# The last chunk's low weights in both halves of the rows, and the first balance's small matmuls inside the projection

## The chip, the cores and the metric

One core of one Trainium2 chip. The metric is the device time of one execution in microseconds (us). Of the kernel before, three runs took 2725.89 to 2726.05 us, median 2726.04.

## The reference

x is 2048 rows of 576. Two attentions with 32 heads of 18 read the same x; a sigmoid gate per row mixes them:

```python
g = _sigmoid((x * gate_w).sum(-1, keepdims=True))
a = _A_ref(x, A_wqkv, A_wo)              # softmax attention, own k and v for each head
b = _B_ref(x, B_wq, B_wk, B_wv, B_wo)    # one k and one v for all heads
return g * a + (1 - g) * b
```

## The kernel before

The work has two parts. The first part projects x with all weights; the second runs, for 64 heads, a pass for the row maxima (L511), the scores with their exponentials (L548, L555) and the product with v (L561), and at times the output projection (L677). The change touches the first part alone.

**Projection.** The weights that act on the columns of q, k, the gate and B's v stand side by side as 14 tiles of 128 columns. x comes transposed, in chunks of 128 of its 576 rows: four full chunks and a last one of 64 rows. A product of two f32 numbers is made of three products of rounded ones: every operand is split into a high part (`h`) and a low part (`l`, the rest). One accumulation over all chunks is written out in `PROJ` (L37): four matmuls high by high, four with low weights by high x, four with high weights by low x, and two for the last chunk. There x keeps its high part in partitions 0 to 63 and its low part in 64 to 127 of the same chunk (L332, L334), and the high weights are written into both halves (L135), so that one matmul on 128 rows gives two of the products. The low weights of that chunk are written into rows 0 to 63 alone (L137), and the fourteenth matmul has 64 rows.

A *job* is one such accumulation for a weight tile and 512 columns of x: 14 tiles by 4 are 56 jobs, number 0 to 55 (`JOBS`). Tiles 0 to 2 come first, in turns over the columns (jobs 0 to 11), then tiles 3 to 13 with four jobs each. Jobs 0 to 2 are made in two halves of 256 columns each, as x arrives. A job writes one bank of PSUM; three banks are named `ps`, four `pm`, and jobs take them by threes (L236). ScalarE and VectorE empty a bank later (`evict`: L248, L251, L254, for some also L257 to L260) into high and low f16 parts, scaled by a column of `tv`; GpSimd issues their transfers. VectorE and ScalarE also split x as it comes (L331 to L334, 256 columns at a time), and split the weights (L133 to L137): for tiles 0 to 2 and v's weights the subtractions are VectorE's, for tiles 3 to 13 they are GpSimd's (`eng_l`).

**Balance.** `tv` comes from the sizes of the weights. For the first three tiles: VectorE measures the weights of five tiles (L173), takes the maximum (`br`, L197); TensorE turns it (L205, the turn of br); VectorE makes `bd` of it (L207 to L210); TensorE spreads `bd` to all partitions (L213); VectorE computes `tv` (L215 to L225). `balance` is a generator with a stop behind `br` and one behind `bd`. It runs beside jobs 3, 4 and 5; the evictions of jobs 0 to 5 follow it. Job 6 uses the bank of job 0 and columns of x that are split behind job 0's eviction. The second balance (`br` at L202) stands around jobs 13 to 15, behind ten measurements of VectorE (L186 to L191).

**V jobs.** 32 projections of A's v (L289, the same fourteen matmuls, 288 columns, x as the stationary operand) end the first part. They alternate with the first max matmuls (L511, 54 rows, alternately in partitions 64 to 117 and 0 to 53).

The engines work through their instructions in the order in which the program writes them.

Of the kernel before, what the change touches and what calls it, by code (L numbers as in the profile page):

```python
# [8 lines left out]
F32 = mybir.dt.float32  # L9
# [5 lines left out]
OP = mybir.AluOpType  # L15
# [9 lines left out]
NKT = 5  # L25
# [9 lines left out]
LEAD = 22  # L35
PRODS = (("h", "h"), ("h", "l"), ("l", "h"))
PROJ = [("h", "h", k, 128) for k in range(NKT - 1)] + [("l", "h", k, 128) for k in range(NKT - 1)] + \  # L37
       [("h", "l", k, 128) for k in range(NKT - 1)] + [("h", "h", NKT - 1, 128), ("l", "h", NKT - 1, 64)]


def q_row(u):
# [8 lines left out]
def gated_mix_kernel(ctx: ExitStack, tc: tile.TileContext, xT, wall, wv, wo, out):  # L50
    nc = tc.nc
# [75 lines left out]
    def load5(t, src, eng=None):  # L127
        dma(t[:, 0:4, :], src[0:512, :].rearrange("(k p) m -> p k m", p=P), eng)
        dma(t[0:64, 4, :], src[512:576, :], eng)

    def split_w(st, w, eng_l):

        nc.scalar.activation(w["h"][:, 0:4], st[:, 0:4], AF.Copy)  # L133
        for b in (0, 64):
            nc.scalar.activation(w["h"][b:b + 64, 4], st[0:64, 4], AF.Copy)  # L135
        eng_l.tensor_tensor(w["l"][:, 0:4], st[:, 0:4], w["h"][:, 0:4].bitcast(F32), op=OP.subtract)
        eng_l.tensor_tensor(w["l"][0:64, 4], st[0:64, 4], w["h"][0:64, 4].bitcast(F32), op=OP.subtract)  # L137

    norm_b = wpool.tile([P, 2, 10], F32, name="norm_b", bufs=1)
    norm_a = wpool.tile([P, (MT - 4) * P], F32, name="norm_a", bufs=1)  # L140
# [19 lines left out]
    def turn_mask():  # L160
        pt = ps_m.tile([P, 512], F32, name="pm")
        for g in range(4):
            nc.tensor.transpose(pt[:, MT * g:MT * g + MT], mask_r[:, g, :], ident[0:MT, 0:MT])
        nc.vector.tensor_copy(mask, pt[:, 0:4 * MT].rearrange("p (g m) -> p g m", m=MT))

    def load_w(mt, eng=None):
        st = wpool.tile([P, NKT, P], F32, name="wst", bufs=MT - 2)
        load5(st, wall[mt], eng)
        return st
# [6 lines left out]
    def measure_b(mt, st):  # L176

        if mt == 0:
            size(norm_b[:, 0, 0:2], st[:, :, ROW_KB:ROW_KB + DH])
        f0, f1 = max(ROW_Q - P * mt, 0), min(ROW_Q + DH * H - P * mt, P)  # L180
        size(norm_b[:, 1, 2 * mt:2 * mt + 2], st[:, :, f0:f1])
# [45 lines left out]
    def prep_w(st, eng=None):  # L227
        w = {y: wpool.tile([P, NKT, P], F32R, name=f"w{y}", bufs=4) for y in "hl"}
        split_w(st, w, eng or nc.gpsimd)
        return w  # L230
# [4 lines left out]
    def bank(odd=False):  # L235
        return ps_m.tile([P, 512], F32, name="pm") if odd else ps_s.tile([P, 512], F32, name="ps")  # L236

    def products(fp, w, s0, a0, b0):
        for n, (a, b, k, kr) in enumerate(PROJ):
            nc.tensor.matmul(fp[:, a0:b0], w[a][:kr, k, :], X[b][:kr, k, s0 + a0:s0 + b0],  # L240
                             start=(n == 0), stop=(n == len(PROJ) - 1), skip_group_check=True)

    def evict(mt, c, fp):
        cs = slice(c * 512, (c + 1) * 512)
        h = stp.tile([P, 512], F16, name="ph")
        l = stp.tile([P, 512], F16, name="pl")
        t = tv[:, mt:mt + 1]
        nc.scalar.activation(h, fp, AF.Copy, scale=t)  # L248
        if mt == 0 or c == 0 and mt in HAS_K:
            st = stp.tile([P, 512], F32, name="pst", bufs=3)  # L250
            nc.scalar.activation(st, fp, AF.Copy)  # L251
            if c == 0:
                KD[mt] = st
        nc.vector.scalar_tensor_tensor(l, fp, t, h, op0=OP.mult, op1=OP.subtract)  # L254
        if c == 1 and mt in HAS_K:
            d = stp.tile([P, 512], F32, name="pd", bufs=1)
            nc.vector.tensor_tensor(d, fp, KD.pop(mt), op=OP.subtract)  # L257
            dh, dl = (stp.tile([P, 512], F16, name=f"pd{y}", bufs=1) for y in "hl")
            nc.scalar.activation(dh, d, AF.Copy, scale=t)
            nc.vector.scalar_tensor_tensor(dl, d, t, dh, op0=OP.mult, op1=OP.subtract)  # L260
        dma(qk_d[0][mt * P:(mt + 1) * P, cs], h, nc.gpsimd)
        dma(qk_d[1][mt * P:(mt + 1) * P, cs], l, nc.gpsimd)
        if c == 1 and mt in HAS_K:
            dma(kd_d[0][mt * P:(mt + 1) * P, :], dh, nc.gpsimd)
            dma(kd_d[1][mt * P:(mt + 1) * P, :], dl, nc.gpsimd)
        if mt == 0:
            dma(z_d[cs], st[ROW_G:ROW_G + 1, :], nc.gpsimd)
            ST[c] = st
# [3 lines left out]
    def shared_v(c):  # L272
        st = ST.pop(c)
        pv = ps_m.tile([P, 512], F32, name="pm")
        for j in range(4):
            nc.tensor.transpose(pv[:, 18 * j:18 * j + 18],
                                st[ROW_VB:ROW_VB + 18, j * P:(j + 1) * P],
                                ident[ROW_VB:ROW_VB + 18, ROW_VB:ROW_VB + 18])
        nc.vector.tensor_copy(vb[:, 4 * c:4 * c + 4, 0:18],
                              pv[:, 0:72].rearrange("p (j d) -> p j d", d=18))  # L280
# [14 lines left out]
    def run(gen):  # L295
        for _ in gen:
            pass
# [6 lines left out]
    def flush():  # L304
        for f in list(late):
            late.remove(f)
            f()

    def project(n, hold=False):

        mt, c = JOBS[n]
        fp = bank(n // 3 % 2)
        products(fp, WP[mt], 512 * c, 0, 512)
        if not hold:
            flush()
        late.append(lambda: evict(mt, c, fp))
        if mt == 0:
            late.append(lambda: late.append(lambda: shared_v(c)))

    with tc.tile_pool(name="xs", bufs=6, side="right") as xsp:  # L320
        XS = []

        def load_x(c, eng=None):
            XS.append(xsp.tile([P, NKT, 256], F32, name="xs"))
            load5(XS[c], xT[:, 256 * c:256 * c + 256], eng)

        def split_x(c):
            xs = XS[c]
            cs = slice(c * 256, (c + 1) * 256)
            xh, xl = X["h"][:, :, cs], X["l"][:, :, cs]  # L330
            nc.scalar.activation(xh[:, 0:4], xs[:, 0:4], AF.Copy)  # L331
            nc.scalar.activation(xh[0:64, 4], xs[0:64, 4], AF.Copy)  # L332
            nc.vector.tensor_tensor(xl, xs[:, 0:4], xh[:, 0:4].bitcast(F32), op=OP.subtract)
            nc.vector.tensor_tensor(xh[64:128, 4], xs[0:64, 4], xh[0:64, 4].bitcast(F32), op=OP.subtract)  # L334

        W = [load_w(0)]
        load_x(0, nc.scalar)
        early = qs[2][:, 0:512]
        nc.vector.memset(early, 0.0)
        nc.scalar.activation(qs[1][:, 0:32], ones, AF.Copy, scale=0.0)  # L340
        for _ in range(18):
            nc.tensor.matmul(acc, early[:, 0:P], early, start=True, stop=True)
        W.append(load_w(1))
        load_x(1)
        W.append(load_w(2))
        for c in (2, 3):
            load_x(c)
        W += [load_w(3), load_w(4)]
        for c in (4, 5):
            load_x(c)  # L350
        WP = [prep_w(W[0], nc.vector)]
        split_x(0)
        for mt in (1, 2):
            WP.append(prep_w(W[mt], nc.vector))
        split_x(1)
        FP = [bank() for mt in range(3)]
        for i in range(2):
            for mt in range(3):
                products(FP[mt], WP[mt], 0, 256 * i, 256 * i + 256)
        for mt in range(3):  # L360
            measure_b(mt, W[mt])
        for c in (2, 3):
            split_x(c)
        turn_mask()
        for c in (6, 7):
            load_x(c)
        for mt in range(5, MT):
            W.append(load_w(mt))
        for mt in (3, 4):
            measure_b(mt, W[mt])  # L370
        project(3, hold=True)
        bal = balance(0)
        for n in (4, 5):
            next(bal)
            project(n, hold=True)
        run(bal)
        for mt in range(3):
            evict(mt, 0, FP[mt])
            if mt == 0:
                for c in (4, 5):  # L380
                    split_x(c)
        flush()
        WP.append(prep_w(W[3]))
        shared_v(0)
        for n in range(6, 12):
            if n == 8:
                for c in (6, 7):
                    split_x(c)
            project(n)
            for mt in range(*AT.get(n, (0, 0))):  # L390
                measure_a(mt, W[mt])
# [355 lines left out]
    at = {}  # L747
# [49 lines left out]
    for T in range(-LEAD, NSTEP + 2, 2):  # L797
# [11 lines left out]
        for op in order.split():  # L809
            k, second, c = op[0], op[1:2] == "B", op[2:]  # L810
# [67 lines left out]
```

## Time and profile before

| | |
|---|---|
| median of 3 runs | 2726.04 us |
| the profiled execution | 2726.16 us, span 2724.3 |
| TensorE busy | 2689.0 us, 99% of the span |
| VectorE | 2421.9 us, 89% |
| ScalarE | 2389.5 us, 88% |
| GpSimd | 285.7 us, 10% |
| mean granted TensorE clock | 0.995 |
| jobs 0 to 55 | 8.96 to 224.68 us |
| V jobs, with the first max matmuls | 224.68 to 306.6 us |

The span goes from the first instruction to the last; the execution's own time has 1.9 us around it. PE is TensorE's matmuls, PEld its weight loads, DVE VectorE, ACT ScalarE, POOL GpSimd. A row of the timeline gives start, duration, engine, line, operation and, for matmuls, rows by columns of the stationary operand and the moving one; rows alike are merged (x4 at the end), and then the duration is that of the whole group. Matmuls are pipelined, so that the durations of neighbours overlap: starts are to be read. In the chain of work that ended last, each piece is what the next one waited for.

### The profile page before, as it was taken

The page shows a single profiled execution, that of the slowest core. Times are in us where ns is not written, and L with a number is a line of the kernel's source. Part 1 is how long each engine was busy: PE and PEld are TensorE (multiplying, and loading weights), DVE is VectorE, ACT ScalarE, POOL GpSimd, SP SyncE. Part 2 cuts the span into 40 slices and gives each one's busy share as a digit, 9 for nine tenths or more (in the row PEclk, how much of TensorE's full clock was granted, in tenths as well). Part 3 has the DMA queues.
Part 4 walks back from the last instruction along what each step waited for, and adds up shares of the span by engine and source line. Part 5 has one row for each costly group of instructions (what it writes and reads, how often), then busy time and mean ns, then how long its engine had stood idle before and what let it go on. Part 6 is the DMA issues. An engine that isn't in the chain of part 4 may idle for free.

```text
span 2724.3 us, 57935 instructions
## 1 busy us (share of the span) xinstructions
PE 2689.0 (99%) x22210; PEld 957.2 (35%) x22210; DVE 2421.9 (89%) x4589; ACT 2389.5 (88%) x4809; POOL 285.7 (10%) x531
## 2 busy tenths in 40 slices
PE   8999999999999999999999999999999999999999
PEld 6767522222222222222222333333333332223444
DVE  6335899999999999999999999999999999998865
ACT  4332599999999999999999999999999999998875
POOL 3641000001000200110110001000100021001000
PEclk9999999999999999999999999999999999999998
DMA  6322100002001100110132113112221112122312
GB/s 188 114 97 85 38 16 19 20 22 59 27 18 32 45 26 17 45 43 20 32 72 80 41 49 97 40 41 57 72 66 48 47 58 64 39 68 85 89 36 95
DMA packets 127089, 150.36 MB, mean 55 GB/s; under 512 B 55339, under 2 KB 94411, under 8 KB 125614
## 3 DMA queue, kind: packets, MB, share of 16 engines
q1 hardware_dynamic: 113628, 121.86, 15.8%
q0 software_dynamic: 7968, 19.23, 2.1%
q10 hardware_dynamic: 5216, 5.57, 0.6%
q8 instruction: 174, 2.85, 0.4%
q14 instruction: 103, 0.84, 0.1%
HBM read 90.89 MB, written 46.45 MB: 50 GB/s over the span
## 4 chain that ended last, share of the span: by engine, by line
ACT 50%; PE 40%; DVE 6%; DMA 2%; issue 1%; SPq 1%; POOL 0%; DVEq 0%; ACTq 0%; POOLq 0%
ACT pt L555 45%; PE acc L561 13%; PE ps L548 11%; ACT xb L514 6%; PE pm L677 4%; PE ps L240 4%; PE pm L240 4%; DVE mx L520 3%; PE ps L289 3%; PE pm L511 1%; SPq L56 1%; DMA R<-r_d 1%; DVE oe L571 1%; DVE junk L517 1%; DVE oacc L731 0%
## 5 line engine op out<-in xcount | busy, mean ns | idle before, releaser
L555 ACT ACTIVATE pt<-ps 128x512 f32<-128x512 f32 x4052 | 2093.2, 637 | 67.8 <-PE pm L511 59.8
L520 DVE TENSOR_REDUCE mx<-pm 128x1 f32<-128x512 f32 x3096 | 1941.4, 683 | 93.6 <-PE pm L511 52.8
L548 PE MATMUL ps<-qs,ksb 56*128 56x512 f16 x2688 | 818.4, 380 | 10.7
L511 PE MATMUL pm<-ksb,qs 54*128 54x512 f16 x2364 | 742.2, 383 | 2.2 <-DVE mx L520 1.1
L561 PE MATMUL acc<-pt,vb 128*19 128x512 f32 (+1 forms) x6136 | 592.2, 458 | 1.9
L561 PE MATMUL acc<-pt,vg 128*19 128x256 f32 (+1 forms) x5664 | 579.5, 481 | 2.3 <-DVE oe L571 0.5
L511 PEld LDWEIGHTS <-qs 54*128 54x128 f16 x4096 | 332.2, 93 | 245.6 <-issue 196.7
L548 PE MATMUL ps<-qs,ksa 56*128 56x512 f16 x1364 | 404.3, 379 | 4.8 <-ACT pt L555 1.3
L548 PEld LDWEIGHTS <-ksb 56*128 56x128 f16 x2688 | 175.0, 94 | 622.1 <-issue 575.8
L511 PE MATMUL pm<-ksa,qs 54*128 54x512 f16 x1232 | 384.8, 382 | 0.5 <-ACT xb L514 0.2
L517 DVE CUSTOM_DVE_ANT_0 junk<-pm,xb 128x512 bf16<-128x512 f32 x500 | 340.6, 681 | 0.0
L514 ACT ACTIVATE xb<-pm 128x512 f32<-128x512 f32 x500 | 316.6, 633 | 0.0
L548 PEld LDWEIGHTS <-ksa 56*128 56x128 f16 x1408 | 89.3, 94 | 328.8 <-issue 298.1
L530 POOL TENSOR_SCALAR mt<-mt 128x32 f32<-128x32 f32 x64 | 18.6, 290 | 1612.0 <-DVE mt L528 1612.0
L561 PEld LDWEIGHTS acc<-pt,vb 128*19 128x19 f32 x6136 | 104.1, 96 | 223.5 <-issue 206.4
L561 PEld LDWEIGHTS acc<-pt,vg 128*19 128x19 f32 x5664 | 96.1, 97 | 222.8 <-issue 204.9
L511 PE MATMUL pm<-kdb,qs 54*128 54x512 f16 x372 | 141.5, 380 | 0.0
L248 ACT ACTIVATE ph<-ps,tv 128x512 f16<-128x512 f32 x29 | 19.8, 686 | 67.3 <-PE ps L240 43.2
L292 ACT ACTIVATE vst<-ps 128x288 f32<-128x288 f32 x32 | 13.2, 412 | 67.4 <-PE ps L289 67.4
L571 DVE COPY oe<-acc 128x512 f32<-128x512 f32 x63 | 43.6, 692 | 30.0 <-PE acc L561 27.9
L248 ACT ACTIVATE ph<-pm,tv 128x512 f16<-128x512 f32 x27 | 18.4, 686 | 54.5 <-PE pm L240 40.6
L254 DVE SCALAR_TENSOR_TENSOR pl<-pm,tv,ph 128x512 f16<-128x512 f32 x27 | 20.1, 749 | 48.8 <-ACT ph L248 38.7
(151 smaller groups left out, 1518.6 us busy)
## 6 DMA issues: line engine op xcount, KB each, us to landing
qs<-qkh SPq DMA_DIRECT2D x244, 72.0 KB
qs<-qkl SPq DMA_DIRECT2D x122, 72.0 KB
onh<-oh SPq DMA_DIRECT2D x32, 256.0 KB
onl<-ol SPq DMA_DIRECT2D x32, 256.0 KB
oih<-onh SPq DMA_DIRECT2D x16, 512.0 KB
oil<-onl SPq DMA_DIRECT2D x16, 512.0 KB
ot<-oe SPq DMA_DIRECT2D x220, 36.0 KB
R<-r_d SPq DMA_DIRECT2D x55, 144.0 KB
```

The source lines that it names most:

```text
L240: nc.tensor.matmul(fp[:, a0:b0], w[a][:kr, k, :], X[b][:kr, k, s0 + a0:s0 + b0], start=(n == 0), stop=(n == len(PROJ) - 1), skip_group_che ...
L248: nc.scalar.activation(h, fp, AF.Copy, scale=t)
L289: nc.tensor.matmul(fp[:, 0:288], X[b][:kr, k, st_ * P:(st_ + 1) * P], w[a][:kr, k, :], start=(n == 0), stop=(n == len(PROJ) - 1))
L511: nc.tensor.matmul(pm, qs[u % 3][b:b + 54, i * P:(i + 1) * P], k, start=True, stop=True)
L514: nc.scalar.activation(MX["x", u, i], pm, AF.Relu)
L517: nc.vector.tensor_tensor_reduce(junk, pm, MX.pop(("x", u, i)), 1.0, -3e38, op0=OP.add, op1=OP.max, accum_out=MX[u][:, i, c:c + 1])
L520: nc.vector.tensor_reduce(MX[u][:, i, c:c + 1], pm, axis=AX.X, op=OP.max)
L548: nc.tensor.matmul(ps, kst(u)[b:b + 56, i * P:(i + 1) * P], qs[u % 3][b:b + 56, c * 512:(c + 1) * 512], start=True, stop=True)
L555: nc.scalar.activation(pt, ps, AF.Exp, scale=SCALE / LIFT ** 2)
L561: nc.tensor.matmul(acc[32 * j:32 * j + 19, a:b], v_of(u, i), PT[u, i, j][:, a:b], start=(i == 0 and a == 0), stop=(i == 15), skip_group_ch ...
L571: nc.vector.tensor_copy(oe, acc)
L677: nc.tensor.matmul(fp[:, 0:288], o[b][:r, t, s2 * P:(s2 + 1) * P], w[a][:r, t, 288 * hf:288 * hf + 288], start=(n == 0), stop=(n == 3 * nt ...
```

## The change

The last line of `PROJ` gets 128 rows instead of 64. In `split_w` the low weights of the last chunk are written twice, into both halves of the rows, both times by VectorE, whoever does the rest. With rows 64 to 127 filled, the fourteenth matmul also adds the product of low weights and low x. The number of matmuls stays. `products` gets a generator and a list of places at which it lets the generator go on. The first balance no longer stands between the jobs: its `br` is emitted ahead of job 3, its turn ahead of job 3's eighth matmul, its spreading and all that follows ahead of job 4's fourth.

```diff
-       [("h", "l", k, 128) for k in range(NKT - 1)] + [("h", "h", NKT - 1, 128), ("l", "h", NKT - 1, 64)]
+       [("h", "l", k, 128) for k in range(NKT - 1)] + [("h", "h", NKT - 1, 128), ("l", "h", NKT - 1, 128)]
...
-        eng_l.tensor_tensor(w["l"][0:64, 4], st[0:64, 4], w["h"][0:64, 4].bitcast(F32), op=OP.subtract)
+        for b in (0, 64):
+            nc.vector.tensor_tensor(w["l"][b:b + 64, 4], st[0:64, 4], w["h"][0:64, 4].bitcast(F32), op=OP.subtract)
...
-    def products(fp, w, s0, a0, b0):
+    def products(fp, w, s0, a0, b0, gen=None, at=()):
         for n, (a, b, k, kr) in enumerate(PROJ):
+            if n in at:
+                next(gen, None)
...
-        project(3, hold=True)
         bal = balance(0)
-        for n in (4, 5):
-            next(bal)
-            project(n, hold=True)
-        run(bal)
+        next(bal)
+        project(3, hold=True, gen=bal, at=(7,))
+        project(4, hold=True, gen=bal, at=(3,))
+        project(5, hold=True)
```

The first place is the first balance on TensorE. Before (names with their numbers: pm_389 is job 4's bank, pm_411 job 5's, br_387 the maximum, bd_409 what VectorE makes of the turn, pm_505 takes turned columns of B's v ahead of job 6):

```order
L240 MATMUL pm_389<-xh_114,wh_208 128x512
L240 MATMUL pm_389<-xh_114,wl_209 128x512
L205 MATMUL pm_404<-ident_87,br_387 2x128
L240 MATMUL pm_411<-xh_114,wh_215 128x512 x4
L240 MATMUL pm_411<-xh_114,wl_216 128x512 x4
L240 MATMUL pm_411<-xl_115,wh_215 128x512 x4
L240 MATMUL pm_411<-xh_114,wh_215 128x512
L240 MATMUL pm_411<-xh_114,wl_216 128x512
L213 MATMUL pm_426<-bd_409,two_121 128x2
L276 MATMUL pm_505<-ident_87,pst_443 128x18 x4
```

The same place of the changed kernel, whose lines are numbered three higher from there on (pm_377 is job 3's bank, pm_399 job 4's, br_375 the maximum, bd_390 what VectorE makes of the turn):

```order
L243 MATMUL pm_377<-xh_114,wl_198 128x512 x3
L206 MATMUL pm_385<-ident_87,br_375 2x128
L243 MATMUL pm_377<-xh_114,wl_198 128x512
L243 MATMUL pm_377<-xl_115,wh_197 128x512 x4
L243 MATMUL pm_377<-xh_114,wh_197 128x512
L243 MATMUL pm_377<-xh_114,wl_198 128x512
L243 MATMUL pm_399<-xh_114,wh_209 128x512 x3
L214 MATMUL pm_403<-bd_390,two_121 128x2
L243 MATMUL pm_399<-xh_114,wh_209 128x512
L243 MATMUL pm_399<-xh_114,wl_210 128x512 x4
```

The turn moved forward by one and a half jobs, into the middle of job 3, the spreading by nearly two, into job 4; job 5 follows without anything between.

The second place is VectorE's queue behind the first balance, at the evictions of jobs 3 to 6. Before:

```order
L260 SCALAR_TENSOR_TENSOR pdl<-pd,tv,pdh 128x512
L254 SCALAR_TENSOR_TENSOR pl<-pm,tv,ph 128x512 x2
L279 COPY vb<-pm 128x4x18 x2
L254 SCALAR_TENSOR_TENSOR pl<-ps,tv,ph 128x512
L186 TENSOR_REDUCE norm_a<-wst 128x128
```

In the changed kernel:

```order
L263 SCALAR_TENSOR_TENSOR pdl<-pd,tv,pdh 128x512
L257 SCALAR_TENSOR_TENSOR pl<-pm,tv,ph 128x512 x2
L138 TENSOR_TENSOR wl<-wst,wh 64x128 x2
L282 COPY vb<-pm 128x4x18 x2
L257 SCALAR_TENSOR_TENSOR pl<-ps,tv,ph 128x512
L187 TENSOR_REDUCE norm_a<-wst 128x128
```

Tile 3's two low writes of the last chunk, one of which was GpSimd's, now stand between the evictions of jobs 5 and 6; such a pair comes once per tile from here on.

More of the change, by code (lines that the diff above doesn't have):

```diff
@@ L307, in flush, with project @@
             f()
-    def project(n, hold=False):
+    def project(n, hold=False, gen=None, at=()):
         mt, c = JOBS[n]
         fp = bank(n // 3 % 2)
-        products(fp, WP[mt], 512 * c, 0, 512)
+        products(fp, WP[mt], 512 * c, 0, 512, gen, at)
         if not hold:
```

## The prediction, made before the changed kernel ran

> **What bounds the kernel now.** I read the chain that ended last first, in order of time, then TensorE's timeline inside one of its pieces, then what the other engines do meanwhile. The chain (start, us, what) from the 45th to the 306th microsecond is TensorE and nothing else:
>
> ```profile
> 195.58 10.94 PE ps L240 x42
> ...
> 232.40 4.51 PE ps L289 x28
> 236.91 0.45 PE pm L511 x3
> 237.35 2.26 PE ps L289 x14
> ```
>
> 42 matmuls are three projection jobs, so a job takes 10.94 / 3 = 3.65 us; a V job takes 2.26, and is followed by either another V job (x28) or four max matmuls (x3, one hidden). In this window the engines PE, PEld, DVE, ACT, POOL were busy for:
>
> ```profile
> 44.61:224.68 180.07, 180.07 (x703) 126.12 (x702) 75.75 (x126) 63.48 (x113) 100.98 (x176) 1.00 0.33 109
> ```
>
> TensorE has no idle time at a granted clock of 1.00, VectorE is busy 42%, GpSimd 56%. What makes a job shorter here shortens the kernel. One job on TensorE (start, us, what):
>
> ```profile
> 202.80 1.20 PE L240 MATMUL ps<-xh,wh 128*128 128x512 f32 x4
> 203.84 1.09 PE L240 MATMUL ps<-xh,wl 128*128 128x512 f32 x4
> 204.77 1.10 PE L240 MATMUL ps<-xl,wh 128*128 128x512 f32 x4
> 205.71 0.39 PE L240 MATMUL ps<-xh,wh 128*128 128x512 f32 x1
> 206.03 0.49 PE L240 MATMUL ps<-xh,wl 64*128 64x512 f32 x1
> 206.44 1.20 PE L240 MATMUL pm<-xh,wh 128*128 128x512 f32 x4
> ```
>
> Read the starts, not the durations, which overlap. Eight 128-row matmuls take 205.71 - 203.84 = 1.87 us, 0.234 each. Around the 64-row one this is broken three times: it starts 0.32 after its predecessor (0.09 too late), the next job starts 0.41 after it (0.18 too late), and that job's first four take 1.04 instead of 0.94 (0.10). Fourteen even steps would be 3.27 us, so 3.65 - 3.27 = **0.37 us a job** hang on the one matmul with 64 rows, or on the change of jobs beside it. The end of the kernel tells these two apart, where three 110-row matmuls make a job and each job has a bank of its own:
>
> ```profile
> 2700.43 0.30 PE L677 MATMUL pm<-woh,endl 110*128 110x288 f32 x1
> ...
> 2706.51 0.29 PE L677 MATMUL pm<-wol,endh 110*128 110x288 f32 x1
> 2706.73 13.13 PE L728 MATMUL pm<-wl,stk 54*128 54x288 f32 x32
> ```
>
> From the first to the second row 46 steps take 6.08 us, 0.132 each, over fifteen changes of bank; the step to 54 rows takes 0.22. So a change of bank costs nothing, a change from over 64 rows to fewer does.
>
> **The change part by part.** All sums go against the profiled execution (2726.16 us, span 2724.3); it stands 0.12 above the median of the runs.
>
> *Rows of the last matmul.* 40 projection jobs lie between the second balance and the V jobs (tiles 4 to 13), all TensorE-bound. They give 40 x 0.37 = **14.9 us**.
>
> V jobs have 288 columns:
>
> ```profile
> 225.31 0.69 PE L289 MATMUL ps<-vwl,xh 128*128 128x288 f32 x4
> 225.84 0.69 PE L289 MATMUL ps<-vwh,xl 128*128 128x288 f32 x4
> ...
> 228.62 0.29 PE L289 MATMUL ps<-vwh,xh 128*128 128x288 f32 x1
> 228.85 0.39 PE L289 MATMUL ps<-vwl,xh 64*128 64x288 f32 x1
> 228.85 0.84 PE L511 MATMUL pm<-ksb,qs 54*128 54x512 f16 x4
> 229.62 0.40 PE L289 MATMUL ps<-vwh,xh 128*128 128x288 f32 x1
> ```
>
> The step is (225.84 - 225.31) / 4 = 0.1325, fourteen are 1.86. A V job followed by a V job takes 4.51 - 2.26 = 2.25, so 0.39 goes; the chain has ten such pairs: **3.9 us**. The other 22 V jobs are followed by max matmuls on 54 rows, and there the change of row count stays. Now the 64-row matmul starts together with the first max matmul, on the other half of the rows, so it is partly free; after the change it costs a step of its own (0.13) and takes its 0.12 (288 columns at the same rate) from ahead of the max matmuls on its half. From 228.62 to 229.62 is 1.00 now; I make it 0.13 + 0.23 + (0.77 - 0.12) = 1.01 then. Bounds: 0.12 less to 0.13 more, 2.6 to 2.9 us over 22 places; I take 0.
>
> *The move from GpSimd to VectorE.* Per operation, ns least, median, most:
>
> ```profile
> L137 POOL TENSOR_TENSOR wl<-wst,wh x11: 465/468/541, 49.6 to 195.6; 64x128 fp32r<-64x128 f32 x11
> L137 DVE TENSOR_TENSOR wl<-wst,wh x3: 276/277/278, 7.9 to 13.0; 64x128 fp32r<-64x128 f32 x3
> ```
>
> GpSimd loses 11 x 0.47 us, VectorE gains 25 x 0.28 for the 14 weight tiles (and two longer ones for V) = 7 us in all. From tile 5 on VectorE's 58% of free time covers them. Tile 3's pair falls into a wait (47.47 below), tile 4's does not.
>
> *The first balance.* VectorE's rows first, with their idle time ahead in brackets, then TensorE's and ScalarE's, then the window with the granted clock as third number from its end:
>
> ```profile
> 21.01 0.42 DVE L334 TENSOR_TENSOR xh<-xs,xh 64x256 fp32r<-64x256 f32 x1
> 21.80 0.22 DVE L164 COPY mask<-pm 128x56 f32<-128x56 f32 x1 [0.38 <-PE pm L163]
> 23.55 0.17 DVE L197 TENSOR_REDUCE br<-norm_b 128x2 f32<-128x20 f32 x1
> 47.47 0.75 DVE L254 SCALAR_TENSOR_TENSOR pl<-ps,tv,ph 128x512 f16<-128x512 f32 x1 [1.05 <-ACT pst L251]
> 52.93 1.23 DVE L333 TENSOR_TENSOR xl<-xs,xh 128x1024 fp32r<-128x1024 f32 x1
> 64.00 0.23 DVE L279 COPY vb<-pm 128x72 f32<-128x72 f32 x1 [1.22 <-PE pm L276]
> 72.56 1.41 DVE L202 TENSOR_REDUCE br<-norm_a 128x1 f32<-128x576 f32 x2
> ```
> ```profile
> 22.73 1.10 PE L240 MATMUL pm<-xh,wl 128*128 128x512 f32 x4
> 32.66 0.38 PE L213 MATMUL pm<-bd,two 2*128 2x2 f32 x2
> 38.46 2.08 PE L240 MATMUL ps<-xh,wh 128*128 128x512 f32 x4 [1.77 <-DVE xl L333]
> ```
> ```profile
> 35.04 0.69 ACT L248 ACTIVATE ph<-ps,tv 128x512 f16<-128x512 f32 x1 [18.05 <-DVE tv L225]
> ```
> ```profile
> 38.46:44.61 6.15, 6.15 (x14) 4.31 (x14) 5.26 (x8) 3.75 (x8) 3.50 (x7) 0.55 0.31 104
> ```
> ```profile
> 75.11 3.46 PE pm L240 x14
> 78.57 0.31 PE pm L213 x2
> 78.88 1.13 PE pm L240 x4
> ```
>
> Now job 6 waits until 38.46, behind tv and the splits of x, and then runs at a clock of 0.55. In the changed kernel the turn of br stands ahead of job 3's eighth matmul, which TensorE would reach at 22.73 + 3 x 0.234 = 23.43 even at the old pace. The six first half jobs save 0.37 each, but VectorE has br only at 23.38 (0.34 sooner, as L164 no longer waits): their 2 us end in a **new wait of TensorE** of about 1.9 us. From there: 0.2 for the turn, 0.1 for the first four, seven steps (1.64): job 4 at 25.4, its fourth matmul and so L213 at 26.1, **6.6 us earlier**. ScalarE's first eviction, and VectorE's queue behind it, move by as much: 28.5. TensorE: job 4 ends at 29.2 (with 0.55 for L213 and its two changes of rows), job 5 at 32.5, turns of v 0.44, job 6 at 32.9. Its inputs are there sooner (the second half of x at 31.8), and the clock has had no reason to fall.
>
> What is late next is VectorE, which was nearly full here. With 3.27 a job and 0.55 where the small turns stand, job 9 begins at 43.8 and its ninth matmul wants the last low x at 45.7; this is ready at 52.93 + 1.23 - 6.6 = 47.6: a wait of 1.9 us. Jobs 9 to 14 then end at 66.0, and the second balance's br is ready at 72.56 + 1.41 - 6.6 = 67.4, less the 1.2 wait that goes at 64.00, plus 0.6 for tile 4's pair: 66.8, a wait of 0.7. Job 15 begins at 67.0 instead of 75.11 and job 16 at 70.6 instead of 78.88: **8.3 us** for all up to there.
>
> Sum: 8.3 + 14.9 + 3.9 = 27.1; 2726.16 - 27.1 = 2699.1, by the median **2699.0 us**. The steps after the 306th microsecond begin earlier and are otherwise as before.
>
> **The rivals.** *Part of the gap stays.* A matmul on all rows could be unable to load its weights while its predecessor on the same rows runs; then the last one of a job pays 126.12 us / 702 = 0.18 for its load (window above) and half of the 0.37 stays: 50 x 0.18 = 9, and 8.3 shrinks to about 7.5, so 2709. Or only the 0.09 ahead of the last matmul goes and the rest comes with the change of job: 50 x 0.09 = 4.5 and 7.5 are won, 2714. Against both: a load of 0.18 beside 512 columns in a step of 0.234 has room only if the two overlap on the same rows, as they do in twelve steps of each job, and the jobs at the end of the kernel change bank and weights without a gap. [...]
>
> *The clock falls in a new wait.* Between 32.66 and 38.46 TensorE did next to nothing, and job 6 paid 6.15 us for what takes 3.65, 2.5 more. The two new waits of 1.9 us are a third as long; if one or both trip the clock: 2701.5 to 2704. [...]
>
> *No gain:* the gaps stay wholly, or VectorE's queue holds job 16 back by as much as TensorE saves; some 5 us are left at most: 2721 to 2728.
>
> [...] From job 16 to the 306th microsecond 209 us remain after the change; a granted clock under 0.87 there costs more than 27 + 5 us; 0.85 would cost 37 and give 2736. Against it: 92% of the rows ran at 1.00 already, and the gapless stretch at 2700 shows no longer steps. [...]
>
> **How the numbers follow.** Forecast 0.80, part of the gap 0.06, clock falls 0.08, no gain 0.04, slower 0.02. The forecast's own range is 2694.5 to 2702.5 (V and max +-2.8, waits of VectorE 0 to 3 us different). To hold 8 in 10 with the fallen clock and the side of the partial gap: 2694 to 2707. A measurement tells 0.2% (5.5 us) from no change: faster 0.94, same 0.04, slower 0.02.
>
> **What would show it.** In the projection every start 0.234 after the last, across jobs, and jobs of 3.27 us in the chain; a 64-row form no longer there. TensorE waiting for br near 21.5 to 23.4, for low x from 45.7 to 47.6, and the clock at 1.00 in the 30s and 40s; ScalarE's first eviction near 28.5 and the first V matmul near 201.5 instead of 224.68. Wrong would be: a gap left at each change of job (first rival), a clock of 0.5 after a wait (second), VectorE waited for in jobs 16 and later, or a clock below 1.00 from 70 to 200.

## The result, and the profile after

The changed kernel takes **2697.21 us** (median of four runs, 2696.39 to 2698.16) beside 2725.97 us for the kernel before on the same chip: a ratio of 0.9896, interval 0.9878 to 0.9913, so 28.8 us faster. Measured twice more, each time beside the kernel before, it took 2698.02 and 2698.32 us (0.9899 and 0.9900); the twelve runs together have a median of 2697.7. Forecast were 2699.0, in a range of 2694 to 2707. The profiled execution took 2698.16 us, its span is 2696.4: 27.9 less than before, where the sum of the prediction said 27.1.

Lines are numbered three higher behind the diff (L243 is the projection, L292 the V jobs, L513 the max matmuls). The timeline of TensorE in the changed kernel, a job of the projection and the job behind it (start, us, what):

```profile
193.83 1.10 PE L243 MATMUL ps<-xh,wh 128*128 128x512 f32 x4
194.76 1.09 PE L243 MATMUL ps<-xh,wl 128*128 128x512 f32 x4
195.70 1.09 PE L243 MATMUL ps<-xl,wh 128*128 128x512 f32 x4
196.63 0.39 PE L243 MATMUL ps<-xh,wh 128*128 128x512 f32 x1
196.86 0.40 PE L243 MATMUL ps<-xh,wl 128*128 128x512 f32 x1
197.10 1.09 PE L243 MATMUL ps<-xh,wh 128*128 128x512 f32 x4
```

All three breaks of the rhythm are gone: from 193.83 to 197.10 are 3.27 us, fourteen steps of 0.234, and the step into the next job (197.10 - 196.86 = 0.24) is no longer than the others, although the bank changes there. The chain of work that ended last, in the changed kernel:

```profile
184.19 9.80 PE pm L243 x42
193.99 6.53 PE ps L243 x28
200.53 3.69 PE ps L292 x28
204.22 0.54 PE pm L513 x4
204.76 2.05 PE ps L292 x14
206.81 0.75 PE pm L513 x4
207.56 3.90 PE ps L292 x28
```

Three jobs take 9.80 us instead of 10.94. A pair of V jobs takes 3.90 instead of 4.51, and the first of them stands at 200.53 instead of 224.75.

From job 3 to job 15 TensorE now waits five times, the first time for the mask's load just ahead of job 3. The rows of its timeline that have idle time ahead (in brackets, with what ended it):

```profile
19.69 0.39 PE L164 MATMUL pm<-ident,mask_r 14*128 14x14 f32 x4 [1.06 <-DMA mask_r<-mask_d]
22.51 0.27 PE L206 MATMUL pm<-ident,br 128*2 128x128 f32 x1 [0.61 <-DVE br L198]
35.82 0.39 PE L279 MATMUL pm<-ident,pst 18*128 18x18 f32 x4 [0.54 <-DVE pd L260]
46.57 1.20 PE L243 MATMUL pm<-xl,wh 128*128 128x512 f32 x4 [1.22 <-DVE xl L336]
65.82 0.27 PE L206 MATMUL pm<-ident,br 128*2 128x128 f32 x1 [0.70 <-DVE br L203]
```

Before, TensorE had two long waits ahead of job 6, 1.77 us for low x and, just ahead of it, 3.24 for pst:

```profile
36.27 0.42 PE L276 MATMUL pm<-ident,pst 18*128 18x18 f32 x4 [3.24 <-ACT pst L251]
```

Both are gone. In their place stand 0.61, 0.54, 1.22 and 0.70, for VectorE each time; the 1.06 is a late load of this execution. None of them costs the clock: the windows of the changed kernel (granted clock third from the end) show 1.00 throughout, here around the 0.54 and the 1.22,

```profile
34.00:36.00 2.00, 1.46 (x9) 0.91 (x8) 1.68 (x3) 0.29 (x1) 1.94 (x4) 1.00 0.87 281
44.00:48.00 4.00, 2.78 (x12) 1.95 (x11) 3.88 (x7) 0.00 (x0) 0.10 (x1) 1.00 0.12 37
```

where the kernel before had 0.55 from 38.46 to 44.61.

One thing must be known before starts are compared. VectorE's first measurement of the weights (norm_b) comes behind loads (ScalarE's split of weights ahead of it, L133, waited 1.48 us for wst before and 1.09 after) and starts at 14.83 to 15.85 us, differently in three executions of one and the same kernel (14.83, 15.78 and 15.66). In the two that are compared here, before first, then after:

```profile
15.74 2.40 DVE L173 TENSOR_REDUCE norm_b<-wst 128x1 f32<-128x72 f32 x8
```
```profile
14.83 2.40 DVE L174 TENSOR_REDUCE norm_b<-wst 128x1 f32<-128x72 f32 x8
```

So 0.91 us of the 27.9 come from an early start of this execution and not from the change. "From norm" below means counted from this row.

### The profile page after: what moved, and what is told of

Same layout as the page of the kernel before. It is cut to its first block, busy times and chain, and to the rows that moved or that the text cites. A ratio compares the mean times of both kernels' runs of the same rounds, so it can differ in the third digit from the quotient of the medians.

```text
span 2696.4 us, 57946 instructions
## 1 busy us (share of the span) xinstructions
PE 2663.0 (99%) x22210; PEld 955.2 (35%) x22210; DVE 2429.9 (90%) x4616; ACT 2389.8 (89%) x4809; POOL 280.0 (10%) x520
## 4 chain that ended last, share of the span: by engine, by line
ACT 51%; PE 40%; DVE 6%; DMA 1%; issue 1%; SPq 1%; DVEq 0%; ACTq 0%
ACT pt L557 45%; PE acc L563 14%; PE ps L550 12%; ACT xb L516 6%; PE pm L679 4%; DVE mx L522 3%; PE pm L243 3%; PE ps L243 3%; PE ps L292 2%; PE pm L513 2%; DVE oe L573 1%; SPq L56 1%; DVE junk L519 1%; DMA xs<-xT 1%; DVE oacc L733 0%
## 5 line engine op out<-in xcount | busy, mean ns | idle before, releaser
L557 ACT ACTIVATE pt<-ps 128x512 f32<-128x512 f32 x4052 | 2095.0, 639 | 69.2 <-PE pm L513 61.2
L522 DVE TENSOR_REDUCE mx<-pm 128x1 f32<-128x512 f32 x3096 | 1941.4, 682 | 89.2 <-PE pm L513 74.9
L513 PE MATMUL pm<-ksb,qs 54*128 54x512 f16 x2364 | 739.7, 383 | 1.9 <-DVE mx L522 1.0
L513 PEld LDWEIGHTS <-qs 54*128 54x128 f16 x4096 | 329.9, 93 | 247.3 <-issue 197.1
L513 PE MATMUL pm<-ksa,qs 54*128 54x512 f16 x1232 | 385.0, 382 | 0.6 <-ACT xb L516 0.4
L513 PE MATMUL pm<-kdb,qs 54*128 54x512 f16 x372 | 141.7, 381 | 0.0
L573 DVE COPY oe<-acc 128x512 f32<-128x512 f32 x63 | 43.6, 692 | 30.0 <-PE acc L563 27.9
```

Source lines behind the costliest of these rows:

```text
L513: nc.tensor.matmul(pm, qs[u % 3][b:b + 54, i * P:(i + 1) * P], k, start=True, stop=True)
L522: nc.vector.tensor_reduce(MX[u][:, i, c:c + 1], pm, axis=AX.X, op=OP.max)
L557: nc.scalar.activation(pt, ps, AF.Exp, scale=SCALE / LIFT ** 2)
L573: nc.vector.tensor_copy(oe, acc)
```

## The experiments

All medians are beside the kernel before in the same set of runs (2725.1 to 2726.0 us).

| run | median us | ratio, interval | job 16 from norm | V from norm |
|---|---|---|---|---|
| before | 2725.97 | | 63.14 | 209.01 |
| changed kernel | 2697.21 | 0.9896, 0.9878 to 0.9913 | 54.83 | 185.70 |
| e1, rows alone | 2702.86 | 0.9917, 0.9904 to 0.9930 | 59.45 | 190.32 |
| e2, balance alone | 2719.73 | 0.9978, 0.9969 to 0.9987 | 57.15 | 203.02 |
| e3, V jobs as before | 2703.07 | 0.9917, 0.9903 to 0.9932 | 54.85 | 185.71 |
| e4, low writes on GpSimd | 2696.97 | 0.9895, 0.9881 to 0.9909 | 54.26 | 185.12 |
| e5, 96 rows | 2698.99 | 0.9902, 0.9886 to 0.9919 | 54.83 | 185.95 |
| e6, 64 rows in ninth place | 2732.60 | 1.0026, 1.0016 to 1.0035 | 63.49 | 209.56 |
| e7, 64 rows in pairs | 2717.32 | 0.9969, 0.9958 to 0.9981 | 61.88 | 200.24 |
| e8, changed kernel again | 2698.02 | 0.9899, 0.9883 to 0.9916 | 55.00 | 185.86 |
| e9, turn four steps later | 2697.54 | 0.9898, 0.9884 to 0.9913 | 54.28 | 185.14 |
| e10, tuned | 2697.22 | 0.9897, 0.9882 to 0.9911 | | 183.79 |
| e11, tuned further | 2694.48 | 0.9888, 0.9871 to 0.9904 | | 182.43 |
| e12, changed kernel, third time | 2698.32 | 0.9900, 0.9885 to 0.9915 | | 185.75 |

The theory is that of the prediction: the gap hangs on the change of row count, and the balance pays through the waits and the clock ahead of job 6. The rivals are that the gap belongs to the change of jobs, or to the last place, and that rows or balance alone would have given all.

**The two parts apart (e1, e2).** Against the kernel before, e1 keeps the balance between the jobs and e2 the 64 rows:

```diff
e1:
-       ... [("h", "h", NKT - 1, 128), ("l", "h", NKT - 1, 64)]
+       ... [("h", "h", NKT - 1, 128), ("l", "h", NKT - 1, 128)]
-        eng_l.tensor_tensor(w["l"][0:64, 4], st[0:64, 4], w["h"][0:64, 4].bitcast(F32), op=OP.subtract)
+        for b in (0, 64):
+            nc.vector.tensor_tensor(w["l"][b:b + 64, 4], st[0:64, 4], w["h"][0:64, 4].bitcast(F32), op=OP.subtract)
e2:
-        project(3, hold=True)
         bal = balance(0)
-        for n in (4, 5):
-            next(bal)
-            project(n, hold=True)
-        run(bal)
+        next(bal)
+        project(3, hold=True, gen=bal, at=(7,))
+        project(4, hold=True, gen=bal, at=(3,))
+        project(5, hold=True)
```

> The row part alone; the first balance stands between the jobs as before. Theory Q (the parts overlap: VectorE's queue sets when job 16 may start, so each part alone is worth more than its share): job 6 still waits for tv and runs at half clock, job 16 starts near 75.3 us (3.6 earlier than in the kernel before), 40 jobs give 15, the V jobs 5: about 2702.5 us. Theory A (the parts add up): the whole gain of 28.8 less the 7.2 of the balance alone: 2704.4 or more.

> The placing of the first balance alone, with 64 rows in the fourteenth matmul and the subtractions on the engines of before. Both theories: job 6 starts near 33.7 us at full clock instead of 38.46 at half, and everything behind it some 7.2 us earlier: about 2718.8 us; steps of 3.65 us a job and 2.26 a V job as before. Under theory Q TensorE waits at the second balance for less than 0.3 us, since it comes there later than in the changed kernel. If the new wait for br or a fallen clock ate the gain: 2722 or more.

The rows alone give 22.65 us (2725.51 - 2702.86), the balance alone 5.78, less than the 7.2 that its expectation had. In e1 the cost that the balance carries is still there, in its chain, its windows and TensorE's timeline:

```profile
36.40 6.05 PE ps L243 x14
```
```profile
36.00:40.00 4.00, 3.60 (x9) 2.83 (x10) 3.87 (x7) 2.86 (x6) 1.25 (x3) 0.50 0.20 66
```
```profile
34.21 0.42 PE L279 MATMUL pm<-ident,pst 18*128 18x18 f32 x4 [3.23 <-ACT pst L254]
36.40 2.07 PE L243 MATMUL ps<-xh,wh 128*128 128x512 f32 x4 [1.77 <-DVE xl L336]
```

Job 6 waits 3.23 and 1.77 us as before and then takes 6.05 us at a clock of 0.50, although a job needs 3.27 otherwise. Up to job 16 the rows bring 3.69 us from norm (63.14 - 59.45), the balance 5.99, both together 8.31: some 1.4 us are paid for twice, since both parts bring TensorE to the same work of VectorE too early. For the last low x (job 9) it waits 0.21 us in e1, 0.54 in e2 and 1.22 in the changed kernel; for the second br 0.70, not at all, and 0.70. In the times, 22.65 + 5.78 = 28.4 beside 28.8 for both (27.1 and 27.4 in the later sets), this overlap can't be seen.

**V jobs alone (e3).** The changed kernel with 64 rows in the last matmul of the V jobs:

```diff
-        for n, (a, b, k, kr) in enumerate(PROJ):
+        for n, (a, b, k, kr) in enumerate(PROJ[:-1] + [("l", "h", NKT - 1, 64)]):
```

> The changed kernel, but V jobs take 64 rows in their fourteenth matmul again. Theory R (the row count alone made the V stage 5.0 us shorter, some of it where max matmuls follow): the V stage goes back from 76.7 to 81.7 us, 2702.2 us. Rival (the forecast: only the ten places where a V job follows a V job count, 3.9 us, the rest is due to something else such as an earlier start): the V stage goes to 80.6, 2701.1 us.

```profile
201.12 4.29 PE ps L292 x28
205.41 0.45 PE pm L513 x3
205.86 2.26 PE ps L292 x14
208.12 0.45 PE pm L513 x3
208.57 4.51 PE ps L292 x28
```

In its chain the pair of V jobs takes 4.51 again. From the first V job to the first scores are 81.70 us, 81.90 in the kernel before and 76.67 in the changed one: 5.0 us hang on these rows, more than the 3.9 of the prediction.

**Who writes (e4).** Both low writes of tiles 3 to 13 go to the engine that does the tile's other subtractions, GpSimd:

```diff
-            nc.vector.tensor_tensor(w["l"][b:b + 64, 4], ...
+            eng_l.tensor_tensor(w["l"][b:b + 64, 4], ...
```

> The changed kernel, but the low weights of the last chunk of tiles 3 to 13 are both written by GpSimd (22 writes of 0.47 us). Theory Q: VectorE's pair of tile 4 (0.6 us) leaves the queue ahead of the second balance, TensorE's wait there shrinks by as much: 2696.6 us. Rival (the writes had to leave GpSimd because its transfers would be late): transfers of the evicted parts start later, banks or buffers come free later, TensorE waits in jobs 16 and later: 2699 us or more.

Job 16 comes 0.6 us sooner from norm (54.26; 54.83 and 55.00 in the changed kernel), the pair of tile 4 that the prediction had put down at 0.6. In the time (2696.97 beside 2697.7 for the twelve runs of the changed kernel, in other sets) it can't be told from the scatter. The rival, transfers that start too late, did not come about; and e4 shows something else behind the first scores, told below.

**What the gap hangs on (e5 to e7).** e5 is the changed kernel with 96 rows in the last matmul; this leaves out the product of the low weights' rows 96 to 127. e6 is the kernel before with the 64-row matmul in ninth place, e7 the kernel before with that matmul first in odd jobs and last in even ones, so that two of them meet:

```diff
e5:
-       ... ("l", "h", NKT - 1, 128)]
+       ... ("l", "h", NKT - 1, 96)]
e6, the second line of PROJ:
-       [("h", "l", k, 128) for k in range(NKT - 1)] + [("h", "h", NKT - 1, 128), ("l", "h", NKT - 1, 64)]
+       [("l", "h", NKT - 1, 64)] + [("h", "l", k, 128) for k in range(NKT - 1)] + [("h", "h", NKT - 1, 128)]
e7:
-        for n, (a, b, k, kr) in enumerate(PROJ):
+        for n, (a, b, k, kr) in enumerate(PROJ[-1:] + PROJ[:-1] if first else PROJ):
```

> The changed kernel with 96 rows in the fourteenth matmul instead of 128 (rows 96 to 127 of that chunk are left out, a part of the product of low weights and low x). Theory H (the gap comes when a matmul uses no more than half of the rows): no gap, 0.234 us a step, 2697 us. Rival (any count other than 128 drains the array): the gaps of 0.37 a job return, about 2720 us.

> The kernel before, with its 64-row matmul in the ninth place of the fourteen instead of the last. Theory S (each change between over 64 rows and fewer costs, wherever it stands): the gaps of 0.09, 0.18 and 0.10 stand around the ninth matmul, none at the change of job, a job keeps 3.65 us; V jobs ahead of max matmuls lose the partly free place of their 64-row matmul and get about 0.3 longer, 22 x 0.3 = 6.6: about 2732 us. Rival J (part of the gap belongs to the change of job): the change of job keeps 0.28 and the ninth matmul adds its own, some 50 x 0.28 more: 2740 us or above.

> The kernel before, with the 64-row matmul first in jobs of odd number and last in even ones, so that two of them follow each other across the change of job. Theory S: one change of rows there and back for two jobs instead of two; in jobs 16 to 55 20 x 0.37 = 7.4 us less, with the earlier ones about 2718 us. Rival L (each 64-row matmul pays by itself, for weights that it can't load ahead): the two still start late one after the other, 2724 us or more.

The timelines of TensorE at a change of jobs, in e5, e6 and e7:

```profile
152.04 0.39 PE L243 MATMUL pm<-xh,wh 128*128 128x512 f32 x1
152.27 0.40 PE L243 MATMUL pm<-xh,wl 96*128 96x512 f32 x1
152.51 1.10 PE L243 MATMUL pm<-xh,wh 128*128 128x512 f32 x4
```
```profile
151.67 0.39 PE L240 MATMUL pm<-xh,wh 128*128 128x512 f32 x1
151.90 1.10 PE L240 MATMUL ps<-xh,wh 128*128 128x512 f32 x4
152.84 1.51 PE L240 MATMUL ps<-xh,wl 128*128 128x512 f32 x5
154.28 1.20 PE L240 MATMUL ps<-xl,wh 128*128 128x512 f32 x4
```
```profile
156.19 0.39 PE L240 MATMUL ps<-xh,wh 128*128 128x512 f32 x1
156.51 0.50 PE L240 MATMUL ps<-xh,wl 64*128 64x512 f32 x1
156.85 0.39 PE L240 MATMUL pm<-xh,wl 64*128 64x512 f32 x1
157.16 1.19 PE L240 MATMUL pm<-xh,wh 128*128 128x512 f32 x4
```

In e6 the change of jobs takes 0.23 us, a plain step, and the gap has gone with the 64 rows: five matmuls from 152.84 to 154.28 take 1.44, 0.27 more than five steps (the row merges the 64-row one with the four before it), and the four behind them take 1.04 instead of 0.94. A job keeps its 3.65. So neither the change of jobs nor the bank costs anything. In e7 one change to 64 rows and back serves two jobs: two jobs take 6.91 us instead of 7.29 (three of its chain 10.36 instead of 10.94), 0.38 saved, and the second 64-row matmul itself comes 0.34 after the first. In e5, 96 rows pass in even steps. The changed row count is the cause by three tests: moved it moves, shared it halves, and it is not any other row count: 96 beside 128 pass without it, 64 beside 128 do not. Where between 64 and 96 rows it begins was not tried.

All three times met the expectation of the theory within 2 us. e6 is 7 us slower than before. Of these, 5.8 arise in the V jobs' stage, which takes 87.7 us instead of 81.9: no 64-row matmul stands beside the max matmuls any longer, as its expectation had it.

**The new waits (e8 to e12).** e8 and e12 are the changed kernel unaltered. e9 puts the turn of br ahead of job 3's twelfth matmul. e10 also splits the last quarter of x ahead of VectorE's measurements and puts the second balance's turn and spreading into job 16. e11 puts that turn ahead of job 15's fourteenth matmul, the spreading ahead of job 16's sixth, and takes e4's writes:

```diff
e9:
-        project(3, hold=True, gen=bal, at=(7,))
+        project(3, hold=True, gen=bal, at=(11,))
e10, beside e9:
-            if n == 8:
+            if n == 7:
...
+            if n == 16:
+                project(n, gen=bal, at=(1, 9))
e11, beside e10:
-            if n == 16:
-                project(n, gen=bal, at=(1, 9))
+            if n in (15, 16):
+                project(n, gen=bal, at=(13,) if n == 15 else (5,))
```

> The changed kernel once more, unchanged, as the measure for the other two of this set: 2697.2 us. Its early loads differ from execution to execution; VectorE's first measurement begins between 14.8 and 15.8 us, whatever the kernel.

> The changed kernel with the turn of br ahead of job 3's twelfth matmul instead of its eighth. Theory Q: TensorE no longer waits for br (0.6 us in the profile), job 4 starts that much sooner and with it tv and all of VectorE's queue: 0.6 to 0.8 us less than the changed kernel in the same set. Rival: VectorE has the turn later and bd is late for the spreading: no gain.

> As e9, and further: the last quarter of x is split ahead of the measurements of tiles 4 and 5 instead of behind them, and the second balance's turn and spreading stand ahead of job 16's second and tenth matmul. Theory Q: the waits of TensorE for low x (1.2) and for the second br (0.7) go as well; no wait over 0.3 us is left from job 3 on, job 16 starts near 66.5 us, 2694.5 us. Rival: VectorE's queue is full, so what it does earlier for x it does later elsewhere; TensorE waits for a bank in jobs 9 to 17 or for the second br inside job 16, and 2696 us or more remain.

> The version with the turn of br ahead of job 3's twelfth matmul, the last quarter of x split ahead of the measurements, both low writes of tiles 3 to 13 by their tile's engine, and now the second balance's turn ahead of job 15's fourteenth matmul and its spreading ahead of job 16's sixth. Theory: the wait of 1.3 us that the version before it showed in job 16 came from the turn standing too early for VectorE's queue behind it; with VectorE's two low writes of a tile out of that queue and the spreading four matmuls after job 16's start no wait over 0.3 us is left there, the first V matmul comes 182.0 to 183.0 us after VectorE's first measurement (185.8 in the changed kernel), and the median is 2694.5. Rival: another operation of VectorE holds the spreading back, the wait stays over 1 us, V comes 183.5 to 184.5 after the measurement and the median is over 2696.

> The changed kernel once more, as the measure for the run beside it: 2697.3, V 185.8 us after VectorE's first measurement under both theories; what differs between its executions is the start of that measurement by some 0.5 us.

e9 wins 0.6 us from norm; in the time it is 0.5 ahead of e8, less than the scatter of either. e10 missed its 2694.5: the wait in job 9 is gone, but TensorE's timeline has a new one,

```profile
70.36 0.38 PE L214 MATMUL pm<-bd,two 2*128 2x2 f32 x2 [1.30 <-DVE bd L211]
```

because VectorE takes up the turned maximum only behind two evictions and tile 5's two low writes, as its timeline shows:

```profile
65.02 1.41 DVE L203 TENSOR_REDUCE br<-norm_a 128x1 f32<-128x576 f32 x2
66.34 1.40 DVE L257 SCALAR_TENSOR_TENSOR pl<-ps,tv,ph 128x512 f16<-128x512 f32 x2
67.66 0.57 DVE L138 TENSOR_TENSOR wl<-wst,wh 64x128 fp32r<-64x128 f32 x2
68.27 0.28 DVE L208 TENSOR_REDUCE bx<-pm 2x1 f32<-2x128 f32 x1
```

In e11 this wait is gone too. Its timeline:

```profile
66.06 0.27 PE L206 MATMUL pm<-ident,br 128*2 128x128 f32 x1
...
67.66 0.38 PE L214 MATMUL pm<-bd,two 2*128 2x2 f32 x2
```

In the chain V starts at 197.74, 182.43 from norm (15.31 in this run), 3.3 us sooner than in e12, as expected. **e11 at 2694.48 us (2693.83 to 2695.74) is the fastest kernel of the study**: its runs do not overlap those of the changed kernel beside it (2697.51 to 2699.16). Of the 3.84 us between them 3.3 are the waits; the rest is spoken of below, with what comes after the first scores.

## Why the prediction was right

*The gap of 0.37 us a job (14.9).* Right in mechanism and size: 40 jobs between job 16 (69.66) and the V jobs (200.53) take 130.87 us, before 145.87 (78.88 to 224.75), 15.0 less. The inference from the kernel's last stage, that a bank costs nothing and fewer rows do, is confirmed by e5, e6 and e7. That holds for 128 rows beside 64 and 110 beside 54; the prediction's bound, over 64 rows to fewer, is the author's inference, and no run places it. The rival by which a load cannot overlap a matmul on the same rows falls with the even steps: from 69.66 to 200.53 TensorE has no idle time, its 563 weight loads, all for 128 rows, take 105.48 of the 130.87 us (0.19 each), and its steps stay at 0.234.

*Up to job 16 (8.3).* Counted from norm 8.31. The path to it held as well. With the 0.91 us of the early start added, the steps came at: ScalarE's first eviction 28.35 (forecast 28.5), job 6 at 32.65 (32.9), low x ready 47.44 (47.6), the second br 66.68 (66.8), job 16 at 70.57 (70.6), the first V job at 201.44 (201.5).

*The waits.* Their ends were right, since VectorE sets them; their lengths depend on when TensorE arrives. The wait for br was 0.61 in the profiled execution, where TensorE had already lost 1.06 to the load of the mask, and 1.80 and 1.66 in e8 and e12: forecast 1.9. The wait for low x was 1.22 to 1.38 instead of 1.9, because job 9 began 0.3 late by the 0.54 at L279, which the prediction lacked: the transposes ahead of job 7 wait for VectorE's pd (L260). The wait at the second br was 0.70, as said. The clock stayed at 1.00 from 20 to 72 us in the changed kernel's first profile, and behind the 1.80 of e8 four matmuls take 0.93 us (23.81 to 24.74), 0.23 a step, so the rival of the fallen clock did not come about. Behind 5 us of waiting (3.23 and 1.77 with four small matmuls between) the clock was 0.50 in e1 (36 to 40 us). How long a wait it takes, the runs do not show. The fall of the clock behind the first scores, below, comes without any such wait.

*V jobs (3.9).* **Mis-sized**: 5.2 (81.90 - 76.67). The ten pairs give their 3.9; the step that failed is the one that set the places with max matmuls at 0. TensorE's timeline there:

```profile
203.79 0.30 PE L292 MATMUL ps<-vwh,xh 128*128 128x288 f32 x1
203.93 0.29 PE L292 MATMUL ps<-vwl,xh 128*128 128x288 f32 x1
204.15 0.61 PE L513 MATMUL pm<-ksb,qs 54*128 54x512 f16 x4
204.69 0.80 PE L292 MATMUL ps<-vwh,xh 128*128 128x288 f32 x4
```

From 203.79 to 204.69 are 0.90 us where the working had 0.13 + 0.23 + 0.65 = 1.01 and before stood 1.00. The fourteenth step (0.14) and the change to 54 rows (0.22) were right; the four max matmuls then need 0.54, not 0.65. The working's own bound of 0.12 less a place covers this; the 0 that it took does not. So each place behind a pair saves 0.1 (0.13 by the chain: 4.51 + 0.45 = 4.96 before, 3.90 + 0.54 = 4.44 after, less the pair's own 0.39); behind a single V job the slot of 2.70 stays at 2.05 + 0.68 = 2.73. There VectorE's four row maxima a slot (0.682 us each, L522) may be what sets the pace; this was not tried.

*What comes after (0).* The prediction let everything behind the 306th microsecond move up unchanged. From the first scores to the end of the span the kernel before takes 2417.65 us, the changed one 2419.2 (277.20 to 2696.4): 1.5 are given back. So the sum closes as 0.91 + 8.31 + 15.0 + 5.2 - 1.5 = 27.9. That the total of 27.1 was so close is partly luck: the 1.3 too little for V and the 1.5 given back nearly cancel, and the early start of norm is in the 27.9.

So this step failed too. Two things give back the 1.5, and marks in ScalarE's work tell them apart: its exponentials (L555, behind the change L557), counted from the first. The 17th stands 13.04 us behind the first scores in the kernel before and 14.02 in the changed one, 1.0 later. From the 501st to the 2001st are 842.88 and 843.67 us, 0.8 more. Some 0.2 come back near the end.

The first is the clock, in windows of 20 us from the first scores, before and after:

```profile
306.65:326.65 20.00, 18.57 (x122) 0.83 0.03 11
```
```profile
277.20:297.20 20.00, 18.97 (x115) 0.74 0.03 11
```

In every run of this study TensorE, which has little to do there (0.38 us of matmul each 0.6 us, between waits of 0.2 for VectorE), falls to a clock of 0.50 a few us behind the first scores. A mean of 0.83 stands for (1 - 0.83) x 2 x 20 = 6.8 us at half rate; the 0.74 are 10.2, read in windows of half a microsecond. The place of the fall goes with the 17th exponential in all fourteen runs: where it came 2.6 to 3.6 us behind the first scores and lasted 6.8 (before, e2, e3, e4, e6, e11), this stands at 12.8 to 13.0; where it came at 4.3 to 5.0 (e1, e5, e7, e9, e10, e12), at 13.4 to 13.8; at 5.5 (e8), or 10.2 long (the changed kernel's first profile), at 14.0. The three profiles of the changed kernel have the fall at 2.5, 4.7 and 5.5, so the kernel does not fix its place. That the place makes the difference is read from the records; no run set it on purpose.

The second belongs to the change. Twice, some 315 and 1070 us behind the first scores, VectorE pauses between two of its own instructions. The first place, before and after:

```profile
620.38 0.22 DVE L526 TENSOR_REDUCE m<-mx 128x16 f32<-128x64 f32 x1
620.70 0.21 DVE L528 STREAM_TRANSPOSE mt<-m 128x32 f32<-128x32 f32 x1
```
```profile
591.91 0.22 DVE L528 TENSOR_REDUCE m<-mx 128x16 f32<-128x64 f32 x1
592.59 0.21 DVE L530 STREAM_TRANSPOSE mt<-m 128x32 f32<-128x32 f32 x1 [0.46 <-DVE m L528]
```

From start to start are 0.32 us before and 0.68 after, and so again at the second place; the other 62 such steps of the changed kernel take 0.33 at most. Both pauses stand in the eight profiles in which VectorE makes the low writes of tiles 3 to 13 (the changed kernel three times, e1, e3, e5, e9, e10), and in none of the other six (before, e2, e4, e6, e7, e11). e4 differs from the changed kernel in these writes alone and has neither pause, so some 0.7 us hang on who writes. Why VectorE pauses is not shown; it has 4616 instructions in the eight, and 4589 or 4594 in the six.

By this e11's lead over e12 has two more parts: it lacks the pauses (0.7, part of the kernel), and in its profile the fall came early (17th exponential at 12.91, in e12 at 13.63), which is luck.

*A clock held down*, which would have made the kernel slower, did not come about: from 70 to 200 us TensorE is busy for all of the 130 us, and the granted clock is 1.00. (The working says that 92% of the rows ran at 1.00 already; by its own fourteen matmuls, one of them half full, it is 13.5 of 14, 96%. No number hangs on it.)

## What to carry to other kernels

Read starts, not durations, at the one instruction of a loop that differs in shape: a matmul of 64 rows among those of 128 saves no time here and cost 0.37 us a job; filling its other rows with another useful product cost TensorE nothing (steps of 0.234), nor did using 96 (0.23 and 0.24). What it costs elsewhere has to be looked for: the low writes that fill the rows cost some 0.7 us behind the first scores as long as VectorE made them. When the pace of an engine improves, look in the queue of the engine that feeds it for the operation that is late next: here TensorE came to wait for VectorE in four places, and e11 won 3.3 us by moving a few small steps of VectorE's, which no faster matmul would have done. And compare starts from a landmark of the same execution, since loads that came early moved everything by up to 1 us (norm_b at 14.83 to 15.85).

## What the runs showed of the hardware

- A change to 64 rows and back cost 0.37 us with 512 columns and 0.39 with 288, so it did not grow with the columns; 96 rows cost nothing (steps of 0.23 and 0.24).
- Two 64-row matmuls in a row share one change, but their step was 0.34 us instead of 0.234 (e7).
- A 64-row matmul ran beside a 54-row one: in the kernel before both start at 228.85. Moving the 64 rows elsewhere cost that stage 5.8 us (e6).
- The granted clock halved for 6.8 us (once 10.2) behind a stretch in which TensorE was busy in pieces (1.53 us of 2.50 in the changed kernel's first profile, 277.20 to 279.70) without an idle time over 0.34 us: so it was not only a long wait that cost the clock. Where it starts differed by 3 us between executions of one kernel.
